# Three of four low parts of the w_out products on VectorE, splits five steps ahead, and half of the next pair's token parts moved into its own first products

## The chip, the cores and the metric

The kernel runs on one core of a Trainium2 chip. The metric is the device time of one execution, in microseconds; lower is better. The engines spoken of are TensorE (PE, the matmuls), VectorE (DVE), ScalarE (ACT), GpSimd (POOL) and SyncE, whose queue (SP) issues the DMAs. Each engine runs its own instructions in the order in which the program wrote them; engines wait for each other at semaphores.

## The reference, cut to what matters

```
x = attention(q, k pooled by 8, v pooled by 8)      # 4608 tokens x 512
x = leaky(x @ w_in) @ w_out                          # first FFN, 512 -> 2048 -> 512
rms = sqrt(mean(x*x, -1) + 1e-6); xn = x / rms * rms_g
out = (silu(xn @ w_gate) * (xn @ w_val)) @ w_out2    # second FFN, 512 -> 1536 -> 512
```

All in 32-bit floats. The change touches the second FFN alone, and in it the last product (with w_out2, "w_out" below).

## The kernel before, in words

**Split products.** A float operand is written as a high part and a low part (`split`, line 92): ScalarE copies the operand into a rounded 32-bit form (the high part), then VectorE or GpSimd subtracts that from the operand (the low part). A product of two operands is three matmuls: high by high, high by low, low by high. So every operand of TensorE costs one ScalarE instruction and, behind it, one VectorE or GpSimd instruction at line 98.

**Pairs.** Tokens go through the second FFN in five pairs of blocks (`second_ffn`, line 1791), q = 2 to 6, with 512, 384, 512, 384 and 512 tokens in each block of a pair. For each pair a fast 2x2 block multiplication is used: seven block products instead of eight, on sums and differences of the blocks. The token operands of it are called B11, B21, T1, T2, T3, T4 and B22 (tiles `xa`, `T`, `xb`); the sums and differences behind T1 to T4 are made by VectorE at line 1092 and the 14 operands (7 names, 2 column halves c) are split by `parts` in `token_steps`. A call with `fine=None` gives the 22 single steps for the pair that follows another pair of the second FFN (four of the five pairs).

**Gate and value products.** For p = 0 to 5 there are two quads, g (gate) and v (value), each with the steps p1, p6, p5, p7, p2, p4, p3 (line 833), in turn for g and v: 14 products for a p, 84 for a pair, each of six matmuls. p7 and p4 add into the bank that p6 filled (`y`), p2 adds into the bank of p1 (`x`), p3 into that of p5 (`w`). Between two of them VectorE must have read the bank: `e6` is the read of `y` after p6, `e7` after p7, `e1` after p4. The results are written as u tiles by VectorE or GpSimd (line 1343).

**w_out products.** Then come 42 steps (`Second.product`): seven block products (A11, S2, S1, S3, A12, S4, A22) with six steps each. `Second.prepare(k)` splits the operand of step k into a tile `b`; the tiles come from four buffers, and right behind `product(k)` stands `prepare(k + 4)`. Its low part is on GpSimd for two k of three and on VectorE for the third. Operands T1 and T2 are VectorE differences (lines 1451 and 1457), T3 and T4 further ones (`combine`, lines 1463 and 1466). `evacuations` read the output banks.

**Norm and token steps.** While pair q runs, the pair q + 1 is loaded (`xst`, line 1024), squared, summed (GpSimd), turned into 1/rms (one product `ms` with ones, a root on ScalarE, reciprocals on VectorE at line 1060) and scaled (line 1064).

**What sets the order.** `at_spot` is a table from a spot to functions. `spot()` is called behind each of the 84 products (spots 0 to 83; a = 84) and each of the 42 steps (from spot 84 on) and writes what is put there. The norm steps stand at spots 12 to 73, the six sums and differences of the tokens at a - 8 to a - 3, their 14 splits and two further differences from a to a + 39, `prepare(0)` to `prepare(3)` at a - 11 to a - 2. There is no other scheduler: the order in the code is the order on each engine.

Of the kernel before, what the change touches and what calls it, by code (L numbers as in the profile page):

```python
# [23 lines left out]
def pooled_attention_then_two_ffns(  # L24
# [67 lines left out]
    def split(hi_eng, hi, lo_eng, lo, src):  # L92

        if hi_eng is nc.scalar:
            nc.scalar.activation(out=hi, in_=src, func=AF.Copy)  # L95
        else:
            hi_eng.tensor_copy(out=hi, in_=src)
        lo_eng.tensor_tensor(out=lo, in0=src, in1=hi.bitcast(F32), op=ALU.subtract)  # L98
# [979 lines left out]
    def token_steps(q, xs, fine):  # L1078

        n = pairs[q][1]  # L1080
        if kinds[q] == 2:
            xs = [[x[:, c, :] for c in range(KC)] for x in xs]
        t = tok[q] = {}
        box = {}
        done = [0]

        def parts(dst, src):
            done[0] += 1
            split(nc.scalar, dst[:, HI, :], nc.gpsimd if done[0] % 3 == 0 else nc.vector, dst[:, LO, :], src)

        def sub(out, u, w):
            nc.vector.tensor_tensor(out=out, in0=u, in1=w, op=ALU.subtract)

        def first(c):
            if c == 0:
                box["a"] = per.tile([P, 2, KC, N], F32R, tag="xhl", bufs=2, name=f"xa{q}")
            t["B11", c] = box["a"][:, :, c, :n]
            t["B21", c] = box["a"][:, :, 2 + c, :n]
            parts(t["B11", c], xs[0][c])

        def t_slot(name, c):
            i = {"T2": 0, "T1": 2, "T3": 4}[name] + c
            t[name, c] = slot("t", i, f"{name}_{q}_{c}")[:, :, :n]
            return t[name, c]

        def sums(c):
            a1, a2, b1, b2 = (xs[z][i] for z in range(2) for i in (c, 2 + c))
            for x in ("T3", "T2"):
                box[x, c] = e_tile(n, f"{x}_{q}_{c}") if kinds[q] == 1 and q else (
                    free_tile(2 * c + (x == "T2"), f"{x}_{q}_{c}")[:, :n]  # L1110
                )
            t3, t2 = box["T3", c], box["T2", c]
            sub(t3, b2, b1)
            sub(b1, b1, a1)
            sub(t2, b2, b1)

        def second(c):
            parts(t_slot("T2", c), box["T2", c])
            parts(t_slot("T1", c), xs[1][c])

        def second_more(c):
            a2 = xs[0][2 + c]
            parts(t["B21", c], a2)
            parts(t_slot("T3", c), box["T3", c])
            sub(a2, a2, box["T2", c])

        def third(c):
            if c == 0:
                box["b"] = per.tile([P, 2, KC, N], F32R, tag="xhl", bufs=2, name=f"xb{q}")
            t["T4", c] = box["b"][:, :, 2 + c, :n]  # L1130
            t["B22", c] = box["b"][:, :, c, :n]
            parts(t["T4", c], xs[0][2 + c])
            parts(t["B22", c], xs[1][2 + c])

        def all_second(c):
            for f in (sums, second, second_more):
                f(c)

        def singles():
            def sum_of(c, k):  # L1140
                a1, b1, b2 = xs[0][c], xs[1][c], xs[1][2 + c]
                if k == 1:
                    return sub(b1, b1, a1)
                x = "T2" if k else "T3"
                box[x, c] = free_tile(2 * c + (k > 0), f"{x}_{q}_{c}")[:, :n]
                sub(box[x, c], b2, b1)

            def part(x, c):
                if x == "-":
                    return sub(xs[0][2 + c], xs[0][2 + c], box["T2", c])  # L1150
                if x == "B11":
                    return first(c)
                if x == "T4" and c == 0:
                    box["b"] = per.tile([P, 2, KC, N], F32R, tag="xhl", bufs=2, name=f"xb{q}")
                if x in ("T4", "B22"):
                    t[x, c] = box["b"][:, :, c + (2 if x == "T4" else 0), :n]
                elif x != "B21":
                    t_slot(x, c)
                src = {"T1": xs[1][c], "B21": xs[0][2 + c], "T4": xs[0][2 + c], "B22": xs[1][2 + c]}
                parts(t[x, c], src[x] if x in src else box[x, c])  # L1160

            order = [(x, c) for x in ("B11", "T2", "T1") for c in (0, 1)]
            order += [(x, c) for c in (0, 1) for x in ("T3", "B21", "-")]
            order += [(x, c) for x in ("T4", "B22") for c in (0, 1)]
            return [lambda c=c, k=k: sum_of(c, k) for c in (0, 1) for k in range(3)] + [
                lambda x=x, c=c: part(x, c) for x, c in order
            ]

        if fine is None:
            return singles()  # L1170

        two = (0, 1)
        early = [lambda c=c: first(c) for c in two]
        for c in two:
            early += [lambda c=c, f=f: f(c) for f in ((sums, second, second_more) if fine else (all_second,))]
        return early, [lambda c=c: third(c) for c in two]
# [252 lines left out]
    class Second:  # L1429
# [38 lines left out]
        def prepare(self, k):  # L1468
            if k >= len(self.steps):
                return  # L1470
            _, x, f = self.steps[k]
            src = {
                "B11": (1, f), "T1": (2, f), "T3": (1, f), "B21": (1, f + HF), "B22": (2, f + HF), "T4": (1, f + HF),
            }.get(x)
            src = up[(self.q, *src)] if src else self.t2[f]
            if k % 4 != 1:
                t = per.tile([P, 2, N], F32R, tag="ghl", bufs=3, name=f"b{self.q}_{k}")
            else:
                t = p2.tile([P, 2, N], F32R, tag="ahl", bufs=1, name=f"b{self.q}_{k}")
            t = self.ready[k] = t[:, :, :self.n]  # L1480
            split(nc.scalar, t[:, HI, :], nc.gpsimd if k % 3 else nc.vector, t[:, LO, :], src)

        def product(self, k):
            w, x, f = self.steps[k]
# [303 lines left out]

    DONE = {"p5": 1, "p2": 0, "p4": 3, "p3": 2}

    def second_ffn(q):
        more = q + 1 < len(pairs)
        xs, norm = norm_steps(q + 1) if more else (None, [])
        second = Second(q)
        at_spot = {}

        def put(i, f, *args):
            at_spot.setdefault(i, []).append(lambda: f(*args))

        a = 14 * NPAIR  # L1800
        for k, f in enumerate(norm):
            put(4 + 5 * k if k < 2 else 12 + 3 * (k - 2) // 2, f)
        for f in range(HF):
            put(a - 34 + 3 * f, second.t1, f)
            put(a - 24 + 3 * f if f < 2 else a - 15 + 3 * f if f < 4 else a - 10 + 3 * f, second.t2_of, f)
            put(a + 4 + 2 * f, second.combine, 3 * HF + f)
            put(a + 28 + f, second.combine, 6 * HF + f)
        for k in range(4):
            put(a - 11 + 3 * k, second.prepare, k)

        if more:
            tokens = []

            def token_step(k):
                if not tokens:
                    tokens.extend(token_steps(q + 1, xs, None))
                tokens[k]()

            for k, i in enumerate((-8, -7, -6, -5, -4, -3, 0, 1, 3, 7, 9, 11, 15, 16, 17, 19, 20, 22, 34, 35, 38, 39)):
                put(a + i, token_step, k)  # L1820

        n = 0

        def spot():
            nonlocal n
            for f in at_spot.pop(n, ()):
                f()
            n += 1

        for p in range(NPAIR):  # L1830
            quads = [Quad(q, p, m) for m in "gv"]
            assert p < 4 or not late_side
            for step in ("p1", "p6", "p5", "p7", "p2", "p4", "p3"):
                for x in quads:
                    getattr(x, step)()
                    if step in DONE:
                        a_done.add((q, p, x.m, DONE[step]))
                    pump()
                    piece()
                    spot()  # L1840
                    tick()
        for k in range(len(second.steps)):
            second.product(k)
            pump()
            second.prepare(k + 4)
            spot()
            left = second.evacuations(k)
            if k + 1 == len(second.steps):
                while left:
                    left.pop(0)()  # L1850
            for i, f in enumerate(left):
                put(n + i, f)
        assert not at_spot
# [49 lines left out]
```

## Time and profile before

| | |
|---|---|
| median of 3 runs | 1775.71 us (1773.09 to 1775.72) |
| the profiled execution, its own time | 1774.06 us |
| its span, first to last instruction | 1772.3 us |
| TensorE busy | 1715.6 us, 97% of the span |
| VectorE busy | 1143.2 us, 65% |
| ScalarE busy | 777.6 us, 44% |
| GpSimd busy | 759.6 us, 43% |
| granted TensorE clock, mean | 0.994 |

The five w_out parts of the second FFN begin at 1066.41, 1218.96, 1387.72, 1539.88 and 1707.85 us. A share of busy time is a mean over stages with different limits, so the w_out parts are read by themselves below. The profile tells the length of an instruction, and in brackets how long the engine stood idle before it and what ended that.

### The profile page before, as it was taken

What the parts mean: (1) busy time and instruction counts of PE and PEld (TensorE: products, weight loads), DVE (VectorE), ACT (ScalarE), POOL (GpSimd) and SP (SyncE); (2) the same over time, 40 slices, a digit from 0 to 9 for tenths busy, and PEclk for the clock granted to TensorE, in tenths of its full rate; (3) what the DMA queues carried; (4) which work ended last, traced back from release to release, by engine and by line L of the source; (5) the groups of instructions that cost most, each with busy time, mean ns of one, the idle gap of its engine ahead of it and who ended that gap; (6) DMA issues with size and microseconds to landing.
All of it is one profiled execution on the core that took longest, in us unless ns stands there. A gap on an engine that the chain in (4) does not pass through costs nothing.

```text
span 1772.3 us, 26910 instructions
## 1 busy us (share of the span) xinstructions
PE 1715.6 (97%) x9412; PEld 1508.2 (85%) x9412; DVE 1143.2 (65%) x1876; ACT 777.6 (44%) x1646; POOL 759.6 (43%) x867
## 2 busy tenths in 40 slices
PE   5799999999999999999999999999999999999999
PEld 4689888888888888888788889998988899998899
DVE  7984546656556554465766679569756975893454
ACT  5664444445454444445544334333433443351133
POOL 5631325646343033344444426434523553371245
PEclk9899999999999999999999999999999999999999
DMA  8542755547667589969987856777766667875573
GB/s 252 181 156 89 266 196 157 177 138 228 194 197 224 194 303 343 323 226 392 320 274 239 301 182 222 244 274 247 229 214 207 203 215 273 286 221 193 169 245 110
DMA packets 227447, 403.39 MB, mean 228 GB/s; under 512 B 59120, under 2 KB 137456, under 8 KB 226800
## 3 DMA queue, kind: packets, MB, share of 16 engines
q1 hardware_dynamic: 227312, 401.67, 68.0%
q8 instruction: 75, 1.23, 0.3%
q14 instruction: 60, 0.49, 0.1%
HBM read 320.34 MB, written 81.26 MB: 227 GB/s over the span
## 4 chain that ended last, share of the span: by engine, by line
PE 80%; DVE 11%; DMA 5%; issue 2%; ACT 1%; SPq 1%; POOL 1%; ACTq 0%; POOLq 0%; DVEq 0%
PE y L643 11%; PE h L597 10%; PE o L1417 8%; PE yg L1311 6%; PE yv L1311 6%; PE yo L1494 5%; PE xv L1311 4%; PE xg L1311 4%; PE wv L1311 4%; PE wg L1311 4%; PE wo L1494 3%; PE xo L1494 3%; PE yh L1311 3%; PE sc L322 2%; PE wh L1311 2%
## 5 line engine op out<-in xcount | busy, mean ns | idle before, releaser
L597 PE MATMUL h<-xhl,w_i 128*128 128x512 f32 (+1 forms) x996 | 250.6, 393 | 6.6 <-DVE ghl L620 5.3
L98 POOL TENSOR_TENSOR b<-u,b 128x512 fp32r<-128x512 f32 (+1 forms) x120 | 165.9, 1394 | 115.7 <-ACT b L95 105.0
L597 PEld LDWEIGHTS h<-xhl,w_i 128*128 128x128 f32 x996 | 176.2, 190 | 36.9 <-DVE ghl L620 5.7
L643 PE MATMUL y<-ghl,w_o 128*128 128x256 f32 (+1 forms) x768 | 153.4, 344 | 0.0
L95 ACT ACTIVATE b<-u 128x512 fp32r<-128x512 f32 (+1 forms) x180 | 105.3, 588 | 88.6 <-PE yo L1494 27.4
L643 PEld LDWEIGHTS y<-ghl,w_o 128*128 128x128 f32 x768 | 117.0, 190 | 12.9 <-POOL w_o L164 0.2
L1343 POOL TENSOR_TENSOR u<-e7v,e7g 128x512 f32<-128x512 f32 (+1 forms) x30 | 38.7, 1291 | 205.6 <-DVE e7v L1282 120.1
L620 DVE TENSOR_TENSOR ghl<-h,ghl 128x512 fp32r<-128x512 f32 (+1 forms) x83 | 55.5, 669 | 87.4 <-ACT h L101 87.3
L643 PE MATMUL y<-ghl,wr 128*128 128x512 f32 x384 | 103.0, 404 | 0.0
L1417 PE MATMUL o<-u,wo 128*128 128x512 f32 x384 | 96.1, 389 | 0.0
L1494 PE MATMUL yo<-ao_S,b 128*128 128x256 f32 x648 | 84.1, 290 | 9.4 <-DVE b L98 9.4
L1494 PEld LDWEIGHTS yo<-ao_S,b 128*128 128x128 f32 x648 | 81.8, 198 | 10.9 <-DVE b L98 10.9
L1417 PE MATMUL o<-ug,wo 128*128 128x512 f32 x384 | 88.7, 389 | 0.0
L1494 PE MATMUL xo<-ao_A,b 128*128 128x256 f32 x648 | 81.3, 284 | 5.1 <-ACT b L95 3.6
L1494 PEld LDWEIGHTS xo<-ao_A,b 128*128 128x128 f32 x648 | 79.3, 192 | 6.8 <-ACT b L95 4.0
L1417 PEld LDWEIGHTS o<-u,wo 128*128 128x128 f32 x384 | 72.1, 188 | 15.0
L1417 PEld LDWEIGHTS o<-ug,wo 128*128 128x128 f32 x384 | 72.1, 188 | 15.0
L1311 PE MATMUL xv<-xa,av 128*128 128x512 f32 (+1 forms) x360 | 83.7, 367 | 0.0
L1311 PE MATMUL xg<-xa,ag 128*128 128x512 f32 (+1 forms) x360 | 83.7, 367 | 0.0
L1311 PE MATMUL yv<-T,av 128*128 128x512 f32 (+1 forms) x360 | 83.7, 367 | 0.0
L1311 PE MATMUL yg<-T,ag 128*128 128x512 f32 (+1 forms) x360 | 83.6, 367 | 0.0
L1494 PE MATMUL wo<-ao_S,b 128*128 128x256 f32 x648 | 80.1, 284 | 1.5 <-DVE b L98 1.5
(212 smaller groups left out, 4031.7 us busy)
## 6 DMA issues: line engine op xcount, KB each, us to landing
ag<-op_g SPq DMA_DIRECT2D x90, 512.0 KB
av<-op_v SPq DMA_DIRECT2D x90, 512.0 KB
ao_S<-op_o SPq DMA_DIRECT2D x60, 512.0 KB
wo<-wo SPq DMA_DIRECT2D x52, 512.0 KB
ao_A<-op_o SPq DMA_DIRECT2D x45, 512.0 KB
wr<-wo SPq DMA_DIRECT2D x32, 512.0 KB
ah<-op_h SPq DMA_DIRECT2D x32, 512.0 KB
k<-in_k_dram SPq DMA_DIRECT2D x40, 256.0 KB
```

The lines of the kernel that those rows point to most:

```text
L95: nc.scalar.activation(out=hi, in_=src, func=AF.Copy)
L98: lo_eng.tensor_tensor(out=lo, in0=src, in1=hi.bitcast(F32), op=ALU.subtract)
L322: nc.tensor.matmul(pt[:, i * n:(i + 1) * n], y[:, p, :], kblk[b % 2][:, p * n:(p + 1) * n], start=True, stop=True,)
L597: nc.tensor.matmul(pt, w[:, sp, c * P:(c + 1) * P], x[c][:, mp, c0:c1], start=c == 0 and i == 0, stop=c == KC - 1 and i == 2,)
L620: nc.vector.tensor_tensor(out=t[:, LO, :], in0=pt, in1=t[:, HI, :].bitcast(F32), op=ALU.subtract)
L643: nc.tensor.matmul(pt, w[:, sp, m * P:(m + 1) * P], g[:, mp, a - c0:a - c0 + n], start=ydone[j, a] == 1 and i == 0 and m % per_bank == 0, ...
L1311: nc.tensor.matmul(pt, wt[:, a, c, sp, :], xt[:, mp, :], start=start and c == 0 and i == 0, stop=c == 1 and i == 2, skip_group_check=not s ...
L1343: eng.tensor_tensor(out=t, in0=src, in1=silu[i, j], op=ALU.mult)
L1417: nc.tensor.matmul(pt, w[:, sp, m * P:(m + 1) * P], u[:, mp, :], start=f == blocks(q, z)[0] and i == 0, stop=f == blocks(q, z)[-1] and i == 2,
L1494: nc.tensor.matmul(pt, u[:, sp, m * P:(m + 1) * P], wt[:, :, mp, :], start=first and f == 0 and i == 0 and m % 2 == 0, stop=f == HF - 1 an ...
```

## The change

Five edits, all in the second FFN:

1. `prepare`: GpSimd takes the low part only where k % 4 == 3, VectorE the rest (before: VectorE where k % 3 == 0).
2. `prepare` runs five steps ahead instead of four, with a fifth buffer (slot "o" 0, which is free there): k % 5 == 1 uses the `ahl` tile, 3 the slot, the rest the three `ghl` tiles. `prepare(0)` to `prepare(4)` stand at a - 18, a - 15, ..., a - 6.
3. `parts` of `token_steps` with `fine=None`: all low parts on VectorE (before: every third on GpSimd).
4. The token steps are moved: the six sums and differences to a - 19, a - 17, ..., a - 9; B11, T2, T1 and T3 to a + 8 to a + 34; B21, the two further differences, T4 and B22 (eight steps) to spots 0 to 7 of the next pair, by the list `carried`.
5. The norm steps are put from spot 14 on, five spots for four steps (before: from 12 on, three spots for two), the two loads at spots 7 and 10 (before 4 and 9); `t2_of` of f = 4 and 5 and `combine` of T3 move by a spot or a few.

```diff
         def parts(dst, src):
             done[0] += 1
-            split(nc.scalar, dst[:, HI, :], nc.gpsimd if done[0] % 3 == 0 else nc.vector, dst[:, LO, :], src)
+            split(nc.scalar, dst[:, HI, :], nc.gpsimd if done[0] % 3 == 0 and fine is not None else nc.vector, dst[:, LO, :], src)
...
-            order += [(x, c) for c in (0, 1) for x in ("T3", "B21", "-")]
-            order += [(x, c) for x in ("T4", "B22") for c in (0, 1)]
+            order += [(x, c) for x in ("T3", "B21", "-", "T4", "B22") for c in (0, 1)]
...
-            if k % 4 != 1:
+            if k % 5 == 1:
+                t = p2.tile([P, 2, N], F32R, tag="ahl", bufs=1, name=f"b{self.q}_{k}")
+            elif k % 5 == 3:
+                t = slot("o", 0, f"b{self.q}_{k}")
+            else:
                 t = per.tile([P, 2, N], F32R, tag="ghl", bufs=3, name=f"b{self.q}_{k}")
...
-            split(nc.scalar, t[:, HI, :], nc.gpsimd if k % 3 else nc.vector, t[:, LO, :], src)
+            split(nc.scalar, t[:, HI, :], nc.gpsimd if k % 4 == 3 else nc.vector, t[:, LO, :], src)
...
+        for i, f in enumerate(carried):
+            put(i, f)
+        carried.clear()
...
-            put(4 + 5 * k if k < 2 else 12 + 3 * (k - 2) // 2, f)
+            put(7 + 3 * k if k < 2 else 14 + 5 * (k - 2) // 4, f)
...
-        for k in range(4):
-            put(a - 11 + 3 * k, second.prepare, k)
+        for k in range(5):
+            put(a - 18 + 3 * k, second.prepare, k)
...
-            for k, i in enumerate((-8, -7, -6, -5, -4, -3, 0, 1, 3, 7, 9, 11, 15, 16, 17, 19, 20, 22, 34, 35, 38, 39)):
+            for k, i in enumerate((-19, -17, -15, -13, -11, -9, 8, 9, 15, 16, 18, 20, 22, 34)):
                 put(a + i, token_step, k)
+            carried.extend(lambda k=k: token_step(k) for k in range(14, 22))
...
-            second.prepare(k + 4)
+            second.prepare(k + 5)
```

**GpSimd in the first w_out steps of a 384 pair (q = 3).** `b_k` is the operand of step k, `T_4_0` and `T_4_1` are token operands of the next pair, `u` are the results of the gate and value products. Before:

```order
L1343 TENSOR_TENSOR u_11_12341<-e7v_5_12338,e7g_5_12323 128x384
L98 TENSOR_TENSOR b_2_12371<-u_2_11759,b_2_12371 128x384
L98 TENSOR_TENSOR b_4_12433<-u_4_11904,b_4_12433 128x384
L98 TENSOR_TENSOR b_5_12450<-u_5_11885,b_5_12450 128x384
L98 TENSOR_TENSOR b_7_12480<-t_3_0_12157,b_7_12480 128x384
L98 TENSOR_TENSOR T_4_0_12483<-T_4_0_12355,T_4_0_12483 128x512
L98 TENSOR_TENSOR b_8_12495<-t_3_2_12315,b_8_12495 128x384
L98 TENSOR_TENSOR b_10_12525<-t_3_4_12467,b_10_12525 128x384
L98 TENSOR_TENSOR b_11_12542<-t_3_4_12467,b_11_12542 128x384
```

Now (the lines after the edits are numbered one lower or higher):

```order
L1342 TENSOR_TENSOR u_11_12355<-e7v_5_12352,e7g_5_12342 128x384
L98 TENSOR_TENSOR b_7_12462<-t_3_0_12161,b_7_12462 128x384
L98 TENSOR_TENSOR b_11_12520<-t_3_4_12479,b_11_12520 128x384
L98 TENSOR_TENSOR b_15_12583<-u_3_11739,b_15_12583 128x384
L98 TENSOR_TENSOR b_19_12643<-u_1_11585,b_19_12643 128x384
```

Between two multiplications of the pairs GpSimd now has one `b` in four and no token operand.

**VectorE in the same pair, from the `e1` of p = 4 to the `e6` of p = 5.** `rms` and `xst` are norm steps of the next pair, `T` <- `xst` and `xst` <- `xst` its sums and differences. Before:

```order
L1282 TENSOR_TENSOR e1g_4_12114<-yg_4_12126,e1g_4_12114 128x384
L1060 RECIPROCAL rms_1_12155<-rms_1_12155 128x128
L1282 TENSOR_TENSOR e1v_4_12124<-yv_4_12135,e1v_4_12124 128x384
L1060 RECIPROCAL rms_1_12155<-rms_1_12155 128x128
L1282 TENSOR_TENSOR e6g_4_12133<-wg_4_12145,e6g_4_12133 128x384
L1282 TENSOR_TENSOR e6v_4_12142<-wv_4_12159,e6v_4_12142 128x384
L1064 SCALAR_TENSOR_TENSOR xst_1_11616<-xst_1_11616,gain,rms_1_12155 128x512 x2
L1282 TENSOR_TENSOR e6g_5_12285<-yg_5_12278,e1g_5_12266 128x384
```

Now:

```order
L1281 TENSOR_TENSOR e1g_4_12119<-yg_4_12133,e1g_4_12119 128x384
L98 TENSOR_TENSOR b_0_12232<-u_0_11608,b_0_12232 128x384
L1281 TENSOR_TENSOR e1v_4_12130<-yv_4_12142,e1v_4_12130 128x384
L1092 TENSOR_TENSOR xst_1_11624<-xst_1_11624,xst_0_11589 128x512
L1281 TENSOR_TENSOR e6g_4_12140<-wg_4_12153,e6g_4_12140 128x384
L1281 TENSOR_TENSOR e6v_4_12149<-wv_4_12163,e6v_4_12149 128x384
L98 TENSOR_TENSOR b_1_12268<-u_1_11585,b_1_12268 128x384
L1092 TENSOR_TENSOR T_4_0_12271<-xst_1_11624 128x512
L1092 TENSOR_TENSOR T_4_1_12291<-xst_1_11624 128x512
L1281 TENSOR_TENSOR e6g_5_12300<-yg_5_12293,e1g_5_12280 128x384
```

The reciprocals and scalings have moved ahead of the first row, and the first splits and the sums and differences of the tokens have come in from behind the last.

**VectorE where one pair ends and the next begins (q = 2 to 3).** `xa` and `xb` are token operands of the pair that begins. Before:

```order
L98 TENSOR_TENSOR xb_11400<-xst_1_9882,xb_11400 128x384 x2
L1282 TENSOR_TENSOR uo_0_10897<-yo_0_10879,uo_0_10897 128x512
L1282 TENSOR_TENSOR uo_1_10919<-yo_1_10880,uo_1_10919 128x512
L1282 TENSOR_TENSOR e6g_0_11543<-yg_0_11536,e1g_0_11525 128x384
L1282 TENSOR_TENSOR e6v_0_11552<-yv_0_11545,e1v_0_11534 128x384
L1282 TENSOR_TENSOR e7g_0_11577<-yg_0_11536,e1g_0_11525 128x384
L1282 TENSOR_TENSOR e7g_0_11577<-wg_0_11554,e7g_0_11577 128x384
L1282 TENSOR_TENSOR e7v_0_11587<-yv_0_11545,e1v_0_11534 128x384
```

Now:

```order
L1281 TENSOR_TENSOR uo_1_10911<-yo_1_10875,uo_1_10911 128x512
L98 TENSOR_TENSOR xa_10928<-xst_0_9852,xa_10928 128x384 x2
L1281 TENSOR_TENSOR e6g_0_11532<-yg_0_11525,e1g_0_11510 128x384
L1092 TENSOR_TENSOR xst_0_9852<-xst_0_9852,T_3_0_10618 128x384
L1281 TENSOR_TENSOR e6v_0_11542<-yv_0_11535,e1v_0_11521 128x384
L1092 TENSOR_TENSOR xst_0_9852<-xst_0_9852,T_3_1_10681 128x384
L98 TENSOR_TENSOR xb_11552<-xst_0_9852,xb_11552 128x384 x2
L1281 TENSOR_TENSOR e7g_0_11570<-yg_0_11525,e1g_0_11510 128x384
L1281 TENSOR_TENSOR e7g_0_11570<-wg_0_11545,e7g_0_11570 128x384
L98 TENSOR_TENSOR xb_11552<-xst_1_9896,xb_11552 128x384
L1281 TENSOR_TENSOR e7v_0_11582<-yv_0_11535,e1v_0_11521 128x384
```

The last token splits now stand between the bank reads of the pair that they serve. On TensorE nothing moves but the two `ms` products of a pair, each by one to six products earlier inside the same pair.

## Rows read from the trace of the kernel before

**Rows 1.** The page's part 1: busy us, share of the span, instructions.

```profile
PE 1715.6 (97%) x9412; PEld 1508.2 (85%) x9412; DVE 1143.2 (65%) x1876; ACT 777.6 (44%) x1646; POOL 759.6 (43%) x867
```

**Rows 2.** Windows of the five w_out parts: length, then busy us of PE, PEld, DVE, ACT, POOL, clock, DMA.

```profile
1066.41:1130.63 64.22, 61.26 (x505) 60.65 (x504) 56.84 (x56) 32.84 (x59) 44.01 (x30) 1.00 0.69 216
1218.96:1272.72 53.76, 48.21 (x380) 47.23 (x379) 49.15 (x58) 29.52 (x59) 38.19 (x30) 0.97 0.78 252
1387.72:1451.56 63.84, 61.22 (x506) 60.62 (x504) 57.05 (x56) 33.07 (x59) 45.01 (x30) 1.00 0.68 217
1539.88:1593.58 53.70, 48.75 (x379) 47.32 (x379) 48.78 (x58) 29.51 (x59) 39.33 (x30) 0.97 0.78 251
1707.85:1768.33 60.48, 60.48 (x505) 60.42 (x503) 27.43 (x38) 26.70 (x44) 35.93 (x26) 1.00 0.51 167
```

**Rows 3.** Timeline, PE, second w_out part: start, length, instruction, [idle before <- releaser].

```profile
1224.17 0.38 PE L1494 MATMUL xo<-ao_A,b 128*128 128x256 f32 x1 [1.82 <-ACT b L95]
...
1230.47 8.10 PE L1494 MATMUL yo<-ao_S,b 128*128 128x256 f32 x53 [2.16 <-DVE b L98]
...
1259.55 6.64 PE L1494 MATMUL wo<-ao_S,b 128*128 128x256 f32 x54
1266.03 6.86 PE L1494 MATMUL yo<-ao_A,b 128*128 128x256 f32 x54
```

**Rows 4.** Window behind the second gap of that part.

```profile
1231.00:1234.00 3.00, 3.00 (x16) 3.00 (x15) 3.00 (x5) 1.00 (x2) 1.29 (x2) 0.50 0.09 34
```

**Rows 5.** Timeline, DVE, last gate and value products of the 384 pair q = 3.

```profile
1204.00 0.94 DVE L1060 RECIPROCAL rms<-rms 128x128 f32<-128x128 f32 x1
1204.86 0.49 DVE L1282 TENSOR_TENSOR e1v<-yv,e1v 128x384 f32<-128x384 f32 x1
...
1209.56 0.74 DVE L1064 SCALAR_TENSOR_TENSOR xst<-xst,gain,rms 128x512 f32<-128x512 f32 x1
1210.22 0.54 DVE L1282 TENSOR_TENSOR e6v<-yv,e1v 128x384 f32<-128x384 f32 x1
...
1211.82 0.55 DVE L1457 TENSOR_TENSOR t<-u,u 128x384 f32<-128x384 f32 x1
1212.28 0.55 DVE L1282 TENSOR_TENSOR e7g<-yg,e1g 128x384 f32<-128x384 f32 x1
1212.87 0.56 DVE L1282 TENSOR_TENSOR e7g<-wg,e7g 128x384 f32<-128x384 f32 x1
...
1219.20 0.68 DVE L1092 TENSOR_TENSOR T<-xst 128x512 f32<-128x512 f32 x1
1219.80 0.55 DVE L1282 TENSOR_TENSOR e1g<-yg,e1g 128x384 f32<-128x384 f32 x1
```

**Rows 6.** Timeline, PE, same stretch: p7 of the last g quad.

```profile
1210.64 1.20 PE L1311 MATMUL yg<-T,ag 128*128 128x384 f32 x6
1211.68 1.20 PE L1311 MATMUL yv<-T,av 128*128 128x384 f32 x6
```

**Rows 7.** Timeline, ACT, same stretch.

```profile
1213.52 0.53 ACT L1335 ACTIVATE e7g<-e7g 128x384 f32<-128x384 f32 x1 [5.17 <-DVE e7g L1282]
1213.95 0.51 ACT L95 ACTIVATE b<-u 128x384 fp32r<-128x384 f32 x1
```

**Rows 8.** Timeline, DVE and POOL at the same time, same pair.

```profile
1200.44 1.02 POOL L1343 TENSOR_TENSOR u<-e7v,e7g 128x384 f32<-128x384 f32 x1 [8.85 <-ACT e7g L1335]
1200.77 1.10 DVE L1457 TENSOR_TENSOR t<-u,u 128x384 f32<-128x384 f32 x1
...
1240.05 1.64 DVE L98 TENSOR_TENSOR b<-u,b 128x384 fp32r<-128x384 f32 x1
```

**Rows 9.** Timeline, DVE and PE, first products of the same pair.

```profile
1139.18 0.55 DVE L1282 TENSOR_TENSOR e7v<-yv,e1v 128x384 f32<-128x384 f32 x1
...
1142.08 1.20 PE L1311 MATMUL yv<-xb,av 128*128 128x384 f32 x6
```

More of the change, by code (lines that the diff above doesn't have):

```diff
@@ L1475, in prepare @@
             src = up[(self.q, *src)] if src else self.t2[f]
-            if k % 4 != 1:
+            if k % 5 == 1:
[3 more added lines that the diff above has]
+            else:
                 t = per.tile([P, 2, N], F32R, tag="ghl", bufs=3, name=f"b{self.q}_{k}")
-            else:
-                t = p2.tile([P, 2, N], F32R, tag="ahl", bufs=1, name=f"b{self.q}_{k}")
             t = self.ready[k] = t[:, :, :self.n]
-            split(nc.scalar, t[:, HI, :], nc.gpsimd if k % 3 else nc.vector, t[:, LO, :], src)
+            split(nc.scalar, t[:, HI, :], nc.gpsimd if k % 4 == 3 else nc.vector, t[:, LO, :], src)
         def product(self, k):
@@ L1789, in pooled_attention_then_two_ffns @@
     DONE = {"p5": 1, "p2": 0, "p4": 3, "p3": 2}
+    carried = []
     def second_ffn(q):
@@ L1798, in put @@
             at_spot.setdefault(i, []).append(lambda: f(*args))
+        for i, f in enumerate(carried):
+            put(i, f)
+        carried.clear()
         a = 14 * NPAIR
         for k, f in enumerate(norm):
-            put(4 + 5 * k if k < 2 else 12 + 3 * (k - 2) // 2, f)
+            put(7 + 3 * k if k < 2 else 14 + 5 * (k - 2) // 4, f)
         for f in range(HF):
             put(a - 34 + 3 * f, second.t1, f)
-            put(a - 24 + 3 * f if f < 2 else a - 15 + 3 * f if f < 4 else a - 10 + 3 * f, second.t2_of, f)
-            put(a + 4 + 2 * f, second.combine, 3 * HF + f)
+            put(a - 24 + 3 * f if f < 2 else a - 15 + 3 * f if f < 4 else a - 1 + f, second.t2_of, f)
+            put(a + 5 + 2 * f - f // 5, second.combine, 3 * HF + f)
             put(a + 28 + f, second.combine, 6 * HF + f)
-        for k in range(4):
-            put(a - 11 + 3 * k, second.prepare, k)
+        for k in range(5):
+            put(a - 18 + 3 * k, second.prepare, k)
         if more:
```

## The prediction

> **What bounds the kernel now.** The order of reading: the busy table, then windows over the five w_out parts, then the timeline of TensorE inside one, then that of VectorE before and in it.
>
> TensorE is busy nearly the whole span, so only its gaps can be won. The windows [rows 2] show where they are: the last w_out part has no gap, 60.48 us long and 60.48 us busy. It has the same products as the other two 512 parts, which take 64.22 and 63.84 us. In the 384 parts a block of 54 matmuls goes by in 6.48 us where nothing waits (1259.55 to 1266.03 [rows 3]), so seven blocks are 45.36 us; they take 53.76 and 53.70 us. The loss against a part without gaps is 3.74 + 8.40 + 3.36 + 8.34 = 23.84 us. That is all there is to win here.
>
> The gaps stand in the first half of a part and are ended by `b`, the operand of the step, from ScalarE or VectorE [rows 3]. In the 384 parts they also cost clock: behind the second gap the granted clock is 0.50, the 1.2 GHz level [rows 4], and 53 matmuls take 8.10 us where 54 take 6.64 [rows 3], some 1.6 us that the 8.40 holds.
>
> Why is `b` late? VectorE comes late into the part. `e1g` of p = 5 runs at 1219.80 [rows 5], but its product p4 is the fourth behind p7, which starts at 1210.64, at 1.04 us a product [rows 6], and so ends at 1214.80 + 1.20 = 1216.0: 3.8 us late, behind the sums and differences of the next pair's tokens. ScalarE then waits for VectorE, and the splits stand behind it. GpSimd makes it worse: where both engines run, a VectorE instruction of 0.55 us takes 1.10 or 1.64 us [rows 5, 8]. VectorE is busy for 49.15 of 53.76 us in the 384 part [rows 2], much of it such waiting. The last part, which has no next tokens, shows 27.43 us.
>
> **The change, part by part.**
>
> *Prices.* From start to start on VectorE [rows 5]: a 384 instruction 0.46 us (say 0.47), one that needs the result just before it 0.59; a 512 one 0.60; a reciprocal 0.86; a 512 scaling 0.66. On ScalarE [rows 7]: an activation 0.43 to the next start, the split's high part 0.51. A collision with GpSimd adds 0.55 (the 1.10 row) to 1.09 (the 1.64 row) to a VectorE instruction [rows 8].
>
> *The w_out part itself (edits 1 to 3).* For 384: VectorE gets 28 of the 37 low parts written inside the part (28 x 0.47 = 13.2), 8 low parts of tokens (4.8), 14 differences (6.6), ten bank reads (at most 6.0) and six instructions left from p = 5 (2.8): 33.4 us of 45.36. GpSimd keeps nine `b` of its 30 instructions there [rows 2]; nine collisions at 1.09 add at most 9.8: 43.2 us, still under the part. For 512, at 0.60 each and 0.47 for the 384 tokens: 16.8 + 3.8 + 8.4 + 6.0 + 3.6 = 38.6, with collisions 48.4 of 60.48.
>
> Five buffers let `prepare(k + 5)` begin when product k ends, four steps before its own: 4 x 1.08 = 4.3 us at 384. ScalarE and VectorE need 0.51 + 0.55 and some 0.1, or 2.2 us with the worst collision. Before, it was three steps (3.2 us), with a GpSimd instruction of 1.0 and more in two of three. With VectorE on time at the start, `b_5` (the first split inside the part) is ready some 2.4 us in and needed at 5.4. So I cost the gaps in the w_out parts at nothing: 23.84 us gone. What would be late next is `b_10`, whose difference needs the last u of p = 5; by the same count it is done near 7.9 us and wanted at 10.8.
>
> *What comes before it (edits 4 and 5).* Here I expect a new wait. The norm steps, the six sums and differences and `b_0` to `b_2` now all stand ahead of p = 5's p7. That p7 adds into the bank that `e6g` must have read, and starts at 1210.64 if nothing waits [rows 6]. (`ms` moves inside the pair and changes no start of p = 5.) In the 384 pairs the tokens that come are 512 wide. From `e6v` of p = 4, whose product ends 17 x 1.04 - 1.20 = 16.5 us before that p7, VectorE has to do: two reciprocals 1.7, four scalings 2.6, four sums 2.4, seven 384 instructions (t1, t2, b) 3.3, ten bank reads 5.0, the `e6g` itself 0.55: 15.55 us. VectorE also stands still: `b_0` comes right behind `e1g`, and ScalarE first does the silu of `e1g` and then the high part of `b_0`: 0.43 + 0.51, about 1.0 us; `b_1` stands so behind `e6g`, with one instruction between, 0.5. Three GpSimd multiplications fall in, two of them on VectorE instructions that collide, 0.6 each: 1.2. Sum 18.25, so p7 waits 1.8 us. From below: no collision and no standing still, 15.55, no wait. From above: three collisions at 1.09, 20.3, a wait of 3.8. I take 1.8 in each of the two 384 pairs: 3.6 us. Behind it VectorE has little to do until w_out and is on time there.
>
> In what the row shows, an instruction issued 0.33 us after GpSimd began lost 0.55 [rows 8]. The Trainium skill (SBUF — State Buffer, Who interferes with whom) says of VectorE instructions with two SBUF inputs that the engine that comes second is blocked for the whole of the other's instruction. By that rule each of the three costs up to 1.02 us, the wait is 3.6 us in a pair, and the end is 3.6 us later than by the row.
>
> In the 512 pairs a product has 512/384 of the columns, an estimate of 1.39 us from [rows 6], so 17 x 1.39 - 1.6 = 22.0 us are there, and the same list with prices of 512 for its 512 instructions, 384 tokens and three reciprocals is 17.8: no wait.
>
> *The start of the next pair.* Eight carried steps come between the bank reads. Before, `e7v` read its bank by 1139.73 and p4 of v needed it at 1142.08 [rows 9]: 2.3 us free. Of the splits, the one of B22 stands ahead of it and waits for ScalarE's silu and high part, about 1.0, and takes 0.5: 0.8 us left. I cost it at nothing; the bound above is a collision, under 1.1, so 0.3 in each 384 pair. The loads of `xst` now wait for the last T4 and B22 splits; the queue has nothing else to issue until p2, and the weights behind them are ten tiles ahead: nothing.
>
> *Sum.* 1774.06 - 23.84 + 3.6 = 1753.8 for an execution like the profiled one. That one lies 1.65 us under the median of the runs shown; for a median I say **1755.5**.
>
> **Rivals.**
>
> *All gaps gone and no new wait.* For it: the lower end of the 384 sum is under the time that is there. Against: `b_0` stands directly behind the silu that it must wait for. 1775.71 - 23.84 = 1751.9.
>
> *The new wait at p7 is long and costs clock.* 3.8 us twice, and the low clock as in [rows 4] 1.6 twice: 10.8 back, 1762.7; with 3 us of gaps left in the w_out parts 1766. For it: two gaps near each other did that before. Against: here it is a single one.
>
> *Only the first waits go.* If the operands of the first steps stay late because ScalarE's order, not VectorE's time, holds them (`b_5` behind the silu of `e6g`), the 1.82 and 2.16 us gaps of the 384 parts stay with their clock, 5.6 each, and half of the 512 loss: 9 us gained, less 3.6: 1770. Against: ScalarE's wait there is for a late VectorE.
>
> *Slower: VectorE becomes the bound of w_out.* GpSimd's quarter collides with everything. At 1.64 [rows 8] for each of 28 low parts a 384 part takes 33.4 - 13.2 + 45.9 = 66 us, 12 more than now; at 1.69 a 512 part 69, 5 more, and the last part, without tokens, 65, 5 more: 39 us slower, 1815. It decides from a mean low part near 1.2 us in the 384 parts, where 0.47 is the price alone. VectorE is already the busier of the two, 65% against 43% [rows 1]. The Trainium skill (Perfetto Trace Analysis, Optimizing Scalar/DVE Operations) advises moving work off a saturated VectorE, the other way round from this edit; it adds that GpSimd shares a read port with it, so that the move may not help. Only the second half fits the 1.10 row.
>
> **Chances.** The forecast (1753 to 1760, a wait of some size) 0.62; no new wait 0.18; long wait 0.10; only the first waits 0.04; slower 0.04; no change, where a new wait eats the gain, 0.02. The range 1750.5 to 1766 holds all but the last three and the noise. Measurement tells 0.2% (3.5 us) from no change: faster 0.92, same 0.03, slower 0.05.
>
> **What would show it.** Right: all w_out windows at 60.5 and 45.4 us, clock 1.00; p7 of p = 5 in the 384 pairs behind `e6g` by 1 to 3 us, and nothing of that in the 512 pairs; VectorE `b` near 0.6 us on average. Wrong: gaps at `b` still in the first two blocks; a gap at p4 or p3 of p = 0; a mean `b` on VectorE over 1.2 us.

## The result and the profile after

| | before | after |
|---|---|---|
| median | 1774.77 us (1773.09 to 1775.72, 4 runs) | 1757.99 us (1755.55 to 1758.71, 4 runs) |
| the profiled execution, and its span | 1774.06, 1772.3 us | 1755.55, 1753.8 us |

The ratio is 0.9904, 95% interval 0.9887 to 0.9921: 16.8 us or 0.96% faster. The forecast for the median was 1755.5, so the measured one is 2.5 us above it. Line numbers of the kernel after are one off those of before; the steps of the quads, p1 to p3, are listed at line 1833 of before, not 833.

The busy table of the page, against [rows 1]: VectorE has 106 instructions more, GpSimd 106 fewer, and VectorE is busy for 18 us less all the same.

```profile
PE 1709.2 (97%) x9412; PEld 1504.8 (86%) x9412; DVE 1125.2 (64%) x1982; ACT 779.8 (44%) x1646; POOL 604.9 (34%) x761
```

The windows over the five w_out parts (columns as in [rows 2]):

```profile
1066.93:1127.41 60.48, 60.48 (x506) 60.47 (x505) 41.52 (x61) 28.84 (x50) 12.06 (x9) 1.00 0.72 230
1218.14:1263.48 45.34, 45.34 (x379) 45.34 (x379) 34.16 (x63) 25.59 (x50) 9.77 (x9) 1.00 0.89 301
1378.49:1438.97 60.48, 60.48 (x506) 60.48 (x505) 41.53 (x61) 28.84 (x50) 12.06 (x9) 1.00 0.72 228
1529.70:1575.06 45.36, 45.36 (x380) 45.36 (x380) 34.17 (x63) 25.59 (x50) 9.77 (x9) 1.00 0.89 302
1689.32:1749.80 60.48, 60.48 (x505) 60.42 (x503) 35.27 (x53) 25.53 (x42) 11.85 (x9) 1.00 0.50 164
```

Length and TensorE's busy time are the same number in each: no gap is left, and the clock is 1.00 throughout. All 23.84 us are gone. The waits of TensorE in the whole second FFN are now one line (total us, times, longest):

```profile
PE yg L1310 <- DVE e6g L1281: 3.8, 2, 1.9
```

That is the p7 of p = 5 in the two 384 pairs. TensorE's timeline there, against [rows 6]; the same rows stand at 1521.03 in the other pair, and none in a 512 pair:

```profile
1206.37 1.21 PE L1310 MATMUL wv<-T,av 128*128 128x384 f32 x6
1209.48 1.33 PE L1310 MATMUL yg<-T,ag 128*128 128x384 f32 x6 [1.90 <-DVE e6g L1281]
1210.75 1.31 PE L1310 MATMUL yv<-T,av 128*128 128x384 f32 x6
1211.90 1.20 PE L1310 MATMUL xg<-xa,ag 128*128 128x384 f32 x6
```

From 1206.37 to 1211.90 three products take 5.53 us where three of 1.04 take 3.12: a wait costs 2.41 us, not only its 1.90, since the two products behind it start 1.27 and 1.15 us apart. The part of gate and value products of the pair is 90.73 us (1127.41 to 1218.14) where before it was 88.33 (1130.63 to 1218.96 [rows 2]).

The whole account by the traces: the first w_out part starts 0.52 us later, the gaps give 23.84 back, the two waits take 2.41 each: -18.5 us, and the span fell by 18.5. Nothing here explains the 0.52 us: in the traces of the fourteen kernels that part starts anywhere from 1065.65 (e9) to 1067.35 us (e1).

VectorE's timeline ahead of that p7, against [rows 5], with GpSimd's at the same time:

```profile
1191.03 0.56 DVE L1281 TENSOR_TENSOR e6v<-yv,e1v 128x384 f32<-128x384 f32 x1
...
1198.41 1.51 DVE L1064 SCALAR_TENSOR_TENSOR xst<-xst,gain,rms 128x512 f32<-128x512 f32 x1
...
1203.59 0.56 DVE L98 TENSOR_TENSOR b<-u,b 128x384 fp32r<-128x384 f32 x1 [1.00 <-ACT b L95]
...
1206.69 1.07 DVE L98 TENSOR_TENSOR b<-u,b 128x384 fp32r<-128x384 f32 x1 [0.54 <-ACT b L95]
1207.68 1.28 DVE L1092 TENSOR_TENSOR T<-xst 128x512 f32<-128x512 f32 x2
1208.88 0.55 DVE L1281 TENSOR_TENSOR e6g<-yg,e1g 128x384 f32<-128x384 f32 x1
...
1216.63 0.54 DVE L1281 TENSOR_TENSOR e1g<-yg,e1g 128x384 f32<-128x384 f32 x1
...
1198.17 1.19 POOL L1342 TENSOR_TENSOR u<-e7v,e7g 128x384 f32<-128x384 f32 x1 [9.64 <-ACT e2g L1334]
...
1206.32 1.02 POOL L1342 TENSOR_TENSOR u<-e6v,e6g 128x384 f32<-128x384 f32 x1 [0.23 <-ACT e6g L1334]
```

VectorE stands still for 1.00 and 0.54 us behind ScalarE, and two instructions collide: the scaling takes 1.51 where it takes 0.74, the split 1.07 where it takes 0.56. The `e1g` of p = 5 now runs 1.51 us ahead of the w_out part (1216.63 against 1218.14); before it ran 0.84 us into it [rows 5].

### The profile page after: what moved, and what is told of

Same layout as the page of the kernel before. It is cut to its first block, busy times and chain, and to the rows that moved or that the text cites. A ratio compares the mean times of both kernels' runs of the same rounds, so it can differ in the third digit from the quotient of the medians.

```text
span 1753.8 us, 26910 instructions
## 1 busy us (share of the span) xinstructions
PE 1709.2 (97%) x9412; PEld 1504.8 (86%) x9412; DVE 1125.2 (64%) x1982; ACT 779.8 (44%) x1646; POOL 604.9 (34%) x761
## 4 chain that ended last, share of the span: by engine, by line
PE 86%; DVE 6%; DMA 3%; issue 1%; ACT 1%; SPq 1%; POOL 1%; POOLq 0%; DVEq 0%; ACTq 0%
PE y L643 11%; PE h L597 10%; PE o L1416 9%; PE yo L1495 7%; PE yg L1310 6%; PE yv L1310 6%; PE wo L1495 4%; PE xo L1495 4%; PE xg L1310 4%; PE xv L1310 4%; PE wv L1310 4%; PE wg L1310 4%; PE yh L1310 3%; PE wh L1310 2%; PE xh L1310 2%; PE sc L322 2%
## 5 line engine op out<-in xcount | busy, mean ns | idle before, releaser
L98 DVE TENSOR_TENSOR b<-u,b 128x512 fp32r<-128x512 f32 (+1 forms) x140 | 98.4, 703 | 52.2 <-ACT b L95 48.2
L98 POOL TENSOR_TENSOR b<-u,b 128x512 fp32r<-128x512 f32 (+1 forms) x40 | 50.8, 1269 | 144.9 <-ACT b L95 142.5
L1495 PE MATMUL yo<-ao_S,b 128*128 128x256 f32 x648 | 79.4, 283 | 0.0
```

The source lines that it names most:

```text
L1495: nc.tensor.matmul(pt, u[:, sp, m * P:(m + 1) * P], wt[:, :, mp, :], start=first and f == 0 and i == 0 and m % 2 == 0, stop=f == HF - 1 an ...
```

## The experiments

Each ratio is to the kernel before, timed beside it on the same chip. e1 to e4, e5 to e8 and e9 to e12 ran on three different chips, so across these groups the ratios are compared. "Edit 5" means its norm steps and loads: the small moves of `t2_of` and `combine` stayed in e3 and are not in e5, e6, e9 and e10.

**e1: the old sharing (edit 1 undone).**

```diff
-            split(..., nc.gpsimd if k % 4 == 3 else nc.vector, ...)
+            split(..., nc.gpsimd if k % 3 else nc.vector, ...)
```

> The changed kernel with edit 1 alone undone: VectorE writes the low part only where k is a multiple of 3, GpSimd the other two of three; five buffers and all moves stay. Theory A (VectorE came late into the w_out part, and it is the moves and the buffers that put it on time): VectorE is on time at the start, GpSimd's low parts of 1.27 and 1.48 us fit under five steps of 1.08 and 1.44; gaps of at most 3 us in all, 1758 to 1761. Theory B (GpSimd's low parts and their collisions made the gaps): the gaps come back for the greater part, 12 us or more, 1770 and up.

1755.0 us, ratio 0.9889 (0.9876 to 0.9902): not slower than the changed kernel; its median is 3.0 us lower, but the two intervals overlap. The waits of TensorE:

```profile
PE yg L1310 <- DVE e6g L1281: 2.1, 2, 1.1
PE xo L1495 <- DVE b L98: 0.8, 2, 0.4
```

With GpSimd writing two of three low parts there is one gap of 0.4 us in each 384 part and none in the 512 parts, and the wait at p7 is 1.0 to 1.1 us, since the list ahead of `e6g` has a VectorE `b` less. Theory B falls; A forecast 3 to 6 us too much. I had left out that the wait shrinks, but by the traces that gives back only 2.1 us, and the two gaps take 1.5 (each 384 part is 46.08 us long): the spans of the two profiled executions differ by 0.2 us. The rest of the 3.0 us lies in executions that have no trace.

**e2: four buffers (edit 2 undone but for the places of the first splits).**

```diff
-            second.prepare(k + 5)
+            second.prepare(k + 4)
```

> The changed kernel with edit 2 alone undone: four buffers, prepare(k + 4), and prepare(0) to prepare(3) at the new places. Theory A: three steps are 3.2 us in the 384 parts, the split takes 0.51 + 0.56 and a GpSimd one 0.51 + 1.0 to 1.5: no gap or gaps of at most 2 us, 1757 to 1760. Rival (the look-ahead is what counts): gaps near 1.8 us come back in the first blocks of both 384 parts, with their clock some 5 us each, 1765 and up.

1757.04 us, ratio 0.9902 (0.9888 to 0.9916): as the changed kernel, and no gap in w_out. With this sharing and these moves the fifth buffer is worth nothing. Its trace shows what the p7 wait can cost besides. In the first 384 pair, TensorE's timeline:

```profile
1208.81 1.31 PE L1310 MATMUL yg<-T,ag 128*128 128x384 f32 x6 [1.89 <-DVE e6g L1281]
1210.09 1.90 PE L1310 MATMUL yv<-T,av 128*128 128x384 f32 x6
1211.79 2.12 PE L1310 MATMUL xg<-xa,ag 128*128 128x384 f32 x6
```

and windows behind the gap (clock in the third column from the end):

```profile
1208.00:1210.00 2.00, 1.19 (x6) 0.99 (x6) 2.00 (x5) 0.00 (x0) 1.15 (x1) 1.00 0.00 0
...
1211.00:1212.00 1.00, 1.00 (x5) 1.00 (x4) 1.00 (x3) 0.00 (x0) 0.00 (x0) 0.50 0.00 0
...
1213.00:1214.00 1.00, 1.00 (x4) 1.00 (x4) 0.97 (x3) 0.38 (x1) 0.03 (x1) 0.50 0.08 16
...
1522.00:1524.00 2.00, 2.00 (x10) 1.73 (x11) 2.00 (x4) 0.00 (x0) 0.26 (x1) 1.00 0.02 6
```

Here the clock is at 0.50, the 1.2 GHz level, behind a single gap of 1.89 us; behind the same gap in the second 384 pair, at 1522, it stays at 1.00. The product part is 92.29 us in the one and 90.72 in the other: 1.6 us for the clock. The trace of e4 shows the same, low behind the wait in the first 384 pair (92.30 us) and not in the second (90.76); in the changed kernel's trace the clock stays at 1.00 behind both.

**e3: the moves undone (edits 4 and 5), the rest kept.** The spots of token and norm steps, and the order of T4 and B22, are those of before; nothing is carried.

> The changed kernel with edits 4 and 5 undone: norm steps, token steps and splits of the next pair at the places that they had before, nothing carried; the new sharing, the five buffers and the token low parts on VectorE stay. Theory A: VectorE comes late into the 384 parts again, as its e1g of p = 5 did by 3.8 us; the first gaps of the 384 parts are back, 4 to 8 us in each, while the wait at p7 (2.4 us in each 384 pair) goes: 1761 to 1770. Theory B: no gap in w_out and no wait at p7, 1753.

1763.1 us, ratio 0.9931 (0.9917 to 0.9944); its six runs lie 8.2 us apart (1757.91 to 1766.08), more than those of any other kernel here, and the trace is of one at 1764.73. Theory A has the size, but the place is another: the 512 parts have no gap, and the large gap of the 384 parts is not the first one but this, by the timelines of TensorE, GpSimd and VectorE:

```profile
1246.35 2.08 PE L1496 MATMUL yo<-ao_S,b 128*128 128x256 f32 x8 [2.69 <-POOL b L98]
...
1239.98 7.27 POOL L98 TENSOR_TENSOR b<-u,b 128x384 fp32r<-128x384 f32 x2 [3.71 <-ACT b L95]
...
1239.41 0.68 DVE L98 TENSOR_TENSOR T<-T,T 128x512 fp32r<-128x512 f32 x1
1240.02 0.55 DVE L98 TENSOR_TENSOR b<-u,b 128x384 fp32r<-128x384 f32 x1
1240.48 0.68 DVE L98 TENSOR_TENSOR xa<-xst,xa 128x512 fp32r<-128x512 f32 x1
...
1244.77 0.68 DVE L1092 TENSOR_TENSOR xst<-xst,T 128x512 f32<-128x512 f32 x1
```

The longest of GpSimd's low parts in this kernel, by the groups of its line (ns, least/median/most):

```profile
L98 POOL TENSOR_TENSOR b<-u,b x40: 997/1294/6312, 1053.8 to 1749.9; 128x512 fp32r<-128x512 f32 x24, 128x384 fp32r<-128x384 f32 x16
```

A low part that takes 1.0 us took 6.3, and so did its twin in the other 384 part: eleven VectorE instructions with two operands in SBUF follow one another without a pause from 1239.41 to 1245.45, each at its usual 0.55 or 0.68 us, and GpSimd gets on only behind the last. This is not so each time. Earlier in the same part two of GpSimd's low parts got in between such instructions, and it was VectorE's next one that took 1.51 and 1.37 us:

```profile
1231.88 1.42 POOL L98 TENSOR_TENSOR b<-u,b 128x384 fp32r<-128x384 f32 x1 [2.35 <-ACT b L95]
1234.76 1.51 POOL L98 TENSOR_TENSOR b<-u,b 128x384 fp32r<-128x384 f32 x1 [1.46 <-ACT b L95]
...
1231.88 0.55 DVE L1463 TENSOR_TENSOR u<-t,u 128x384 f32<-128x384 f32 x1
1232.35 1.51 DVE L98 TENSOR_TENSOR T<-xst,T 128x512 fp32r<-128x512 f32 x1
...
1234.71 0.68 DVE L98 TENSOR_TENSOR T<-xst,T 128x512 fp32r<-128x512 f32 x1
1235.32 1.37 DVE L98 TENSOR_TENSOR b<-u,b 128x384 fp32r<-128x384 f32 x1
```

What decides between the two is not shown. Six of the eleven are token steps of the next pair (T3, B21 and the two further differences), which edit 4 takes out of this place. Theory A also had the wait at p7 gone; what is left of it is 0.17 us at p7 of g and 0.56 at p7 of v.

**e4: token low parts on GpSimd again (edit 3 undone).**

```diff
-            split(..., nc.gpsimd if done[0] % 3 == 0 and fine is not None else nc.vector, ...)
+            split(..., nc.gpsimd if done[0] % 3 == 0 else nc.vector, ...)
```

> The changed kernel with edit 3 alone undone: every third low part of the next pair's tokens is written by GpSimd. Theory A: four to six GpSimd instructions more in a pair, some of which collide and cost VectorE 0.55 to 1.09 each where it has 11 us to spare in a 384 part: within 0.2% of the changed kernel, 1756 to 1759. Theory B: each collision delays a b, gaps of 0.5 to 1 us in the 384 parts, 1759 to 1762.

1756.98 us, ratio 0.9901 (0.9888 to 0.9914), no gap in w_out, both p7 waits of 1.90 us: edit 3 is worth nothing, as A says.

**e5: the moves alone (edits 4 and 5 on the kernel before).**

> The kernel before with edits 4 and 5 alone (norm steps, token steps and splits of the next pair at their new places, eight carried into its first products); four buffers, GpSimd with two of three low parts, tokens too, as before. Theory A (VectorE on time at the start of the part is what removes the gaps): w_out gaps of 0 to 3 us in all, the wait at p7 of the 384 pairs 0 to 1.1 us since b_1 is GpSimd's: 1754 to 1759. Theory B (each half of the change removes a share, sharing and moves both needed): half of the 23.8 us stays, 1763 to 1768.

1751.89 us, ratio 0.9869 (0.9854 to 0.9885): 22.9 us faster than before, and faster than the whole change. Its waits of TensorE:

```profile
PE yo L1493 <- POOL b L98: 0.5, 2, 0.2
```

Theory A has it, and the gain is even 2 us beyond its range: GpSimd still writes two of three low parts, four buffers are enough, and what stays of the gaps is 0.23 us in each 384 part, which is 46.03 us long, 0.69 more than without a gap:

```profile
1215.92:1261.95 46.03, 45.80 (x379) 45.45 (x379) 33.29 (x45) 26.54 (x52) 34.37 (x28) 1.00 0.87 299
```

The other 0.46 us are slower matmuls behind the gap at a granted clock of 1.00, so they are not the clock's (the text for e9 below calls them so). There is no wait at p7, since `b_0`, prepared at a - 11, stands behind `e6g` on VectorE.

**e6: the sharing alone (edit 1 on the kernel before).**

> The kernel before with edit 1 alone: VectorE writes three of four low parts in the w_out parts. Theory A: VectorE stays late into the 384 parts and gets more to do there, gaps of 4 to 8 us in each remain, those of the 512 parts (3.74 and 3.36) may go: 1763 to 1776. Theory B (GpSimd's collisions made the gaps): most of the 23.8 us goes, 1752 to 1758. Theory C (VectorE becomes the bound): slower than before.

1766.7 us, ratio 0.9953 (0.9941 to 0.9966): theory A. TensorE in the second part, and VectorE's `e1g` of p = 5:

```profile
1223.72 0.39 PE L1494 MATMUL xo<-ao_A,b 128*128 128x256 f32 x1 [2.20 <-ACT b L95]
1224.80 5.92 PE L1494 MATMUL xo<-ao_A,b 128*128 128x256 f32 x26 [0.69 <-POOL b L98]
...
1219.36 0.54 DVE L1282 TENSOR_TENSOR e1g<-yg,e1g 128x384 f32<-128x384 f32 x1
```

The part starts at 1218.14, so `e1g` comes 1.22 us into it, no earlier than before; the first gap stays, with 0.69 us right behind it, the later ones are gone, and the part is 51.63 us long (53.76 before). The 512 parts keep about half of their loss, at 62.41 us. VectorE as the bound (theory C) falls.

**e7: the first five splits behind p7.** `prepare(0)` to `prepare(4)` at a - 8, -6, -4, -2, -1 in the changed kernel.

> The changed kernel with prepare(0) to prepare(4) moved from a-18, -15, -12, -9, -6 to a-8, -6, -4, -2, -1, behind p7 of p = 5. Theory L (the wait at p7 is the length of VectorE's list ahead of e6g of p = 5, and b_0 to b_2 with their 1.5 us of standing still are 3 us of it): no wait at p7, product part of the 384 pairs 88.3 us, 4.8 us less than the changed kernel, 1750 to 1753; unless b_0 to b_4 come late into w_out, then a gap of 1 to 2 us at the part's start. Theory G (a GpSimd collision or e6g's own product sets it): the wait stays at 1 us and more, 1754 to 1757.

1757.7 us, ratio 0.9903 (0.989 to 0.9917). The wait at p7 is gone and the product part is 88.32 us, so theory L holds for it; but the splits now come late into w_out, in all five parts:

```profile
PE xo L1495 <- POOL b L98: 3.9, 5, 1.0
PE xo L1495 <- ACT b L95: 1.2, 2, 0.6
```

The five parts are 6.9 us longer together, which uses up the 4.8 us gained ahead of them.

**e8: the norm steps earlier, at 12 + k.**

> The changed kernel with the norm steps put at 12 + k in place of 14 + 5(k - 2)/4, so that the last reciprocals and scalings stand some ten spots earlier, where VectorE has idle time. Theory L: 2 reciprocals and 4 scalings, 4.4 us, leave the list ahead of e6g, no wait at p7, 1749 to 1753. Theory S (the wait is b_0 and b_1 standing behind ScalarE's silu, in whatever stretch): 1 us or more of the 1.9 stays, 1753 to 1757.

1751.63 us, ratio 0.9869 (0.9855 to 0.9882). No wait at p7 of p = 5 though `b_0` to `b_2` stand where they stood, and VectorE stands still for them as long as before (1.00 and 0.54 us): theory L, the length of the list, not the standing still alone. The waits that are left, 0.40 and 0.48 us, are at p7 of p = 4:

```profile
PE yg L1310 <- DVE e6g L1281: 0.9, 2, 0.5
```

**e9: the moves, five buffers and the old sharing.** The kernel of e5 with `prepare(k + 5)` and the first five splits at a - 11, -8, -5, -2, -1.

> The kernel before with edits 4, 5 and the five buffers of edit 2, but with prepare(0) to prepare(4) at a-11, -8, -5, -2, -1 and the old sharing (GpSimd two of three low parts). Theory L (with the moves VectorE is on time, and what is left is one gap of 0.23 us and its clock in each 384 part, 0.68 us, which a step more of look-ahead covers): no gap in w_out, no wait at p7: 1749.1 for an execution, 1750.5 as median, 1.4 us under the moves alone. Rival (the look-ahead adds GpSimd's collisions earlier in the part, or b_4 holds VectorE behind ScalarE's silu): gaps of 0.3 to 1 us at the start of the parts, 1752 to 1756.

1750.21 us, ratio 0.9865 (0.9852 to 0.9879), theory L; no wait of TensorE in the second FFN. The windows of its first two w_out parts:

```profile
1065.65:1126.13 60.48, 60.48 (x506) 60.47 (x504) 38.02 (x44) 29.91 (x52) 39.05 (x28) 1.00 0.69 230
1214.61:1259.95 45.34, 45.34 (x379) 45.34 (x379) 37.81 (x44) 26.27 (x52) 35.35 (x28) 1.00 0.87 302
```

GpSimd is busy for 35.35 of 45.34 us there and nothing waits. This version beats both kernels: its interval lies below that of the change (0.9887 to 0.9921), by the ratios 6.9 us. Against the moves alone (e5, 0.9869) it is 0.7 us by the ratios, inside their intervals.

**e10: the norm steps closer, alone (edit 5 on the kernel before).**

> The kernel before with edit 5 alone: norm steps closer, the token steps where they were. Theory N (the last reciprocals and scalings ahead of a-11 were what made VectorE late): the 384 gaps of 8.4 us shrink to 0 to 4 each, 1760 to 1767. Theory T (it is the sums, differences and splits of the tokens around the part's start): the gaps stay within 1 us of before, 1773 to 1776; the closer norm steps only make the moved token steps possible.

1774.0 us, ratio 0.9999 (0.999 to 1.0008): theory T. The 384 parts are 53.39 and 53.38 us long. So of the moves those of the token steps must count. That they need the norm steps to end before them is argued from the order; edit 4 without edit 5 was not run.

**e11: the first splits at a - 11, -8, -5, -2, -1 in the changed kernel.**

> The changed kernel with prepare(0) to prepare(4) at a-11, -8, -5, -2, -1 in place of a-18, -15, -12, -9, -6; all else stays, the new sharing too. Theory P (the early places of the first splits, with VectorE standing behind the silu, make the wait at p7): no wait at p7, product part of the 384 pairs 88.3 us; b_3 is GpSimd's and comes some 3 us later than in the changed kernel, a gap of 0 to 0.7 us before it, 1750 to 1754. Theory V (VectorE's greater share makes the wait): 1 us of wait stays, 1754 to 1757.

1750.67 us, ratio 0.9867 (0.9852 to 0.9882): theory P. No wait at p7 and no gap in w_out, with VectorE's greater share left as it is. VectorE stands still behind ScalarE here too,

```profile
1211.63 0.56 DVE L98 TENSOR_TENSOR b<-u,b 128x384 fp32r<-128x384 f32 x1 [1.06 <-ACT b L95]
```

but behind `e6g`, where it costs 0.4 us and not 2.4: the product part is 88.72 us, against 88.32 without any wait.

**e12: the norm steps between, at 13 + 9(k - 2)/8.**

> The changed kernel with the norm steps at 13 + 9(k - 2)/8, between its own 14 + 5(k - 2)/4 and the 12 + k that left a wait of 0.4 us at p7 of p = 4. Theory L: the crowd ahead of p7 is spread over p = 4 and p = 5 and neither p7 waits: product part 88.3 to 88.6 us, 1749.5 to 1751 as median. Rival: both wait, 0.3 to 1 us each, 1752 to 1755.

1754.47 us, ratio 0.9889 (0.9876 to 0.9903): my theory missed, the rival has it. The crowd is not spread, it moves as a whole to p7 of p = 4 and is longer there than with the norm steps earlier:

```profile
PE yg L1310 <- DVE e6g L1281: 2.2, 2, 1.1
```

Its VectorE has four reciprocals and two scalings in the 8.4 us ahead of that `e6g`; the two scalings, 0.66 us each from start to start where nothing disturbs them, take 2.15 us together.

## Why the prediction was right, point by point

- **The gaps go: right in size (23.84 us), the cause only in part.** The prediction put it down to edits 1 to 3 with VectorE on time. The moves alone take nearly all of it (e5), the sharing alone a third of it (8.1 us, e6), edits 1 to 3 without the moves half (11.5 us, e3), edit 5 alone nothing (e10); with the moves in place edit 1, the fifth buffer of edit 2 and edit 3 can each be undone without loss (e1, e2, e4). The step "VectorE comes late into the part" holds for before and e6; in e3 the same token work did its harm later, by a GpSimd low part held up for 5 us, which the prediction did not have. Edit 4 does two things at once, it puts VectorE on time and takes eight token steps out of the w_out part; no run parts the two.
- **VectorE's load in w_out: right.** 34.16 us in the 384 part, where I had 33.4 to 43.2; 41.52 in the 512 part, where I had 38.6 to 48.4. So the slower rival fell: the mean `b` on VectorE is 0.70 us over both widths, median 0.56 in the 384 part.
- **The new wait at p7: right in place, pairs and cause, 1.8 us forecast.** TensorE stands idle for 1.90 us, and p7 starts 2.07 late (3.11 behind the product before it, where 1.04 is usual). Its terms as well: 1.0 and 0.5 us of standing still (1.00, 0.54), two collisions of 0.6 (0.77 and 0.51 by the rows above). Mis-sized is what it costs: 2.41 us with the slow products behind it, 1.2 us more for the two than the sum has. With the first part 0.52 us late, for which the prediction has no term, that is the whole difference between the sum, 1753.8, and the profiled execution, 1755.55. That this one meets the 1755.5 forecast for a median is chance: it lies 2.4 us under its own median, where the forecast had added 1.65. The Trainium skill's rule that the second engine is blocked for the whole of the other's instruction (SBUF — State Buffer, Who interferes with whom) agrees with the scaling at 1198.41, which ends 0.56 us behind GpSimd's end at 1199.36; the wait of 3.6 us that came from it did not come, since only two of the three held VectorE up, for 0.77 and 0.51 us.
- **"Here it is a single one", against the clock's fall: wrong.** e2 shows the fall behind one gap of 1.89 us, and none behind its twin; e4 does the same. The other three runs of the changed kernel have spans of 1756.0 to 1757.0 us, 2.2 to 3.2 over the profiled one, about one or two such falls. They have no trace, and the runs of the kernel before spread as far (1773.28 to 1775.83 beside e9 to e12), so this is one possible cause and not shown.
- **The carried steps cost nothing: right.** TensorE waits nowhere in the first products of a pair.

What edits 1 to 3 added to the moves: the early places of the first splits (edit 2) make the wait at p7, as e11 shows, together with the norm steps beside them, as e8 shows: moving either one removes it. VectorE's greater share lengthens it, as e1 shows. Without the wait the change would stand at 1750.7 (e11).

## What to carry to other kernels

When an operand is late, look for the work that stands ahead of it on its engine before changing who makes it or how many buffers it has: here the places of the next pair's norm and token steps were worth 22.9 us (e5), and a fifth buffer, with the old sharing or the new, at most 1 to 2 us on top, which is not clear of the noise (e9, e11). Without these moves the other three edits were worth 11.5 us (e3), so they are another way to half of the gain and add little to the first. A split that waits for another engine should not stand ahead of a bank read that TensorE awaits; seven spots later it cost 0.4 us (e11), ten spots later it was late itself (e7). Moving a crowd by a few spots moves the wait with it.

## What the runs showed of the hardware

- A GpSimd subtraction of 1.0 us took 6.3 while VectorE ran eleven two-operand instructions without a pause, none of which was slowed, in both 384 parts of e3; elsewhere in that trace GpSimd got in behind a single one, and the next of VectorE's was slowed.
- A gap of TensorE of 1.89 or 1.90 us brought the 1.2 GHz level for some 3 us (1.6 us lost) in two of six cases, and in the same execution not behind the twin gap (the changed kernel, e2, e4); without it, the first two products behind the gap are 1.27 and 1.15 us apart in place of 1.04.
